# Blocked-cache attention on one core: K in loads of eight units, one more unit of lead for the scores, and a new order of copies and loads

## The chip, the core and the metric

The kernel runs on one core of one Trainium2 chip. The core has five engines with a queue of their own each: TensorE (PE; the profile shows its weight loads apart, as PEld), VectorE (DVE), ScalarE (ACT), GpSimd (POOL) and SyncE (SP), and 16 DMA engines beside them. In this kernel SP issues every transfer. TensorE works through its queue in order: an instruction that waits holds back all that stand behind it. The metric is the time of one launch in microseconds (us) on the device. Of each kernel there are several timed runs, whose median counts, and one execution that was profiled.

## What is computed

Two attention problems, A and B, of the same sizes, whose outputs are joined along the last axis:

```python
# B, Sq, D = 16, 144, 448;  H, Sk, Dh = 16, 512, 256;  bfloat16
q = (x @ wq).reshape(B, Sq, H, Dh).transpose(0, 2, 1, 3)
scores = einsum("bhqd,bhkd->bhqk", q, k_cache) * Dh ** -0.5
p = softmax(scores, axis=-1)
o = einsum("bhqk,bhkd->bhqd", p, v_cache)
out_A = o.transpose(0, 2, 1, 3).reshape(B, Sq, H * Dh) @ wo
```

Each of the 2 x 16 x 16 = 512 pairs of batch and head is called a unit here, numbered U = 0 to 511.

## The kernel before

A Python loop over a step number i writes out the program of every engine by hand. A small class, `_Sched`, keeps for each tile who wrote and read it last and puts in the waits. One step holds the stages of several units, each ahead of the last stage by a fixed lead: at step i the loop emits Q of unit i + LQ, the scores of unit i + LS, the transposes of unit i + LT, and PV of unit i. LQ is 22, LS is 13, LT is 2. The stages of a unit are:

- `t_q` (L333): eight TensorE matmuls make q, transposed, in the PSUM tile qp_ps; DVE or ACT scales it into qt_sb (L345, L349).
- 144 query rows do not fit 128 partitions. Rows 0 to 111 (QA) of each unit are its main part; the last 32 rows of four units together are one "remainder" block of 128 rows. `t_sb` (L359) makes the remainder's scores of eight units at once, in the two tiles sb_ps, at every eighth step (phase 0, where (i + 14) % 8 is 0).
- `t_sa` (L435): two matmuls of 512 columns make the main part's scores of one unit in sa_ps. There are two such tiles, each one PSUM bank.
- Softmax of the main part: DVE takes the negated maximum from sa_ps (`t_max`, L446); ACT takes the exponential from sa_ps with the row sum (`t_exp`, L457, an ACTIVATE and an ACTIVATION_READ_ACCUMULATOR); one step later DVE takes the reciprocal (L467) and POOL normalises P (`t_norm`, L475).
- `t_ta` (L488): four PE transposes turn P of one unit around. They write to the same two PSUM tiles as the scores, under the name pta_ps, bitcast to bfloat16; DVE copies them to pt_sb (`t_evac_pta`, L498).
- The remainder's P is normalised on POOL (L400), transposed by a DMA from pb_sb to pbt_sb (`t_ptb_dma`, L410, called pb below), and copied by POOL into pt_sb (`t_copy_ptb`, L421), four units at a time.
- `t_pv` (L521): eight matmuls with V; ACT copies the result into a ring of output columns (L536, L538).
- `t_op_piece` (L559): the output projection, in chunks of 128 rows, two matmuls a piece, is queued behind PV as a chunk becomes complete and spread over the steps by a credit counter; it starts at step OP_FROM of each problem.

Which of the two score tiles a stage uses is said by the unit's number alone, and the main loop of a step emits them in this order:

```python
bank = U % 2        # in t_sa, t_max, t_exp, and also in t_ta and t_evac_pta
...
u = i + LS          # then t_sa(u), t_max(u), t_exp(u)
u = i + LS - 1      # then t_recip(u), t_norm(u)
u = i + LT          # then t_ta(u), t_evac_pta(u)
```

On TensorE a step is so: Q, (every eighth step the remainder's scores), SA, TA, PV, OP.

Transfers are planned in a list, `dma_plan`, of (step, function); they are emitted on SP's one queue when the loop gets to that step, and wait there in order. K comes by transposing DMAs of four units (1 MB) into one of four slots (`t_load_k`, L309); V by loads of four units into one of five slots (L318); x for two batches (L289, L290; the first batch alone ahead, L299, L300); Wq in four parts (L267, L269) and Wo in eight (L277) for each problem. A K slot is free when the scores of its last unit are done.

Of the kernel before, what the change touches and what calls it, by code (L numbers as in the profile page):

```python
# [5 lines left out]
BF16 = mybir.dt.bfloat16  # L6
# [6 lines left out]
PE, ACT, DVE, POOL, SP = "pe", "act", "dve", "pool", "sp"  # L13
# [109 lines left out]
def bass_concat_heads__mha_block_cached__gqa_block_cached__near_ridge_kernel(  # L123
# [13 lines left out]
    xs = (A_x, B_x)  # L137
    ks = (A_k_cache, B_k_cache)
# [4 lines left out]
    Bn, SQ, D = A_x.shape  # L143
    H, SK, DH = A_k_cache.shape[1], A_k_cache.shape[2], A_k_cache.shape[3]
# [3 lines left out]
    NU = Bn * H  # L148
    NT = NP * NU
# [8 lines left out]
    NWG = NWO // WOG  # L158
    NPC = NWO // OPP

    LQ, LS, LT = 22, 13, 2
    LSB = 14
    NKH, NV, NXG = 4, 5, 2
    WO_AT = ((10, 21), (21, 25))
    OP_FROM = (22, 26)
    XB = 2
    assert Bn % XB == 0
    NQT, NPA, NPB, NPT, NST, NSTB, NOST = 12, 13, 2, 8, 4, 2, 3
    NPBT = 1
    RS = 4  # L170
    RC = RS * 128
# [7 lines left out]
    with contextlib.ExitStack() as es:  # L179
        def sb(name, shape, dt):  # L180
            return es.enter_context(nc.sbuf_tensor(name, shape, dt))
# [4 lines left out]
        wq_sb = sb("wq_sb", [128, 4, H * DH], BF16)  # L186
        wo_sb = sb("wo_sb", [128, NWO, D], BF16)
        ring = sb("ring", [128, NWO, RC], BF16)
        kt_sb = sb("kt_sb", [128, NKH, 2, 4 * SK], BF16)
        v_sb = sb("v_sb", [128, NV, 4, 4 * DH], BF16)  # L190
        xt_sb = sb("xt_sb", [128, NXG, 4, XB * SQ], BF16)
        qt_sb = sb("qt_sb", [128, NQT, 2, SQ], BF16)
# [13 lines left out]

        S = _Sched()
        sem_names = list(COMPUTE)
        for i in range(NKH):
# [5 lines left out]
        sem_names.append("xf")  # L215
        for i in range(HG):
            sem_names.append("wq%d" % i)
        for i in range(NWG):
# [63 lines left out]
        def t_load_x(XG):  # L282
            pr, j = divmod(XG, Bn // XB)
            sl = XG % NXG
            x = xs[pr][j * XB:(j + 1) * XB].rearrange("b q d -> (b q) d")
            o = SQ if XG == 0 else 0

            def e(q):
                q.dma_start_transpose(xt_sb[:, sl, 0:3, o:XB * SQ], x[o:XB * SQ, 0:384]).then_inc(sems["xt%d" % sl], 16)  # L289
                return q.dma_start_transpose(xt_sb[:, sl, 3, o:XB * SQ], x[o:XB * SQ, 320:448]).then_inc(  # L290
                    sems["xt%d" % sl], 16)
            S.add(SP, e, writes=[(("xt", sl, f), XG) for f in range(2) if XG > 0 or f > 0], dma_sem="xt%d" % sl,
                  n_dma=2, name="x%d" % XG)

        def t_load_x_first():
            x = xs[0][0]

            def e(q):
                q.dma_start_transpose(xt_sb[:, 0, 0:3, 0:SQ], x[:, 0:384]).then_inc(sems["xf"], 16)  # L299
                return q.dma_start_transpose(xt_sb[:, 0, 3, 0:SQ], x[:, 320:448]).then_inc(sems["xf"], 16)  # L300
            S.add(SP, e, writes=[(("xt", 0, 0), 0)], dma_sem="xf", n_dma=2, name="xf")

        def t_load_k(KH):
            pr, r0 = divmod(4 * KH, NU)
            sl = KH % NKH
            src = ks[pr].rearrange("b h k d -> (b h k) d")[r0 * SK:(r0 + 4) * SK, :]

            def e(q):
                return q.dma_start_transpose(kt_sb[:, sl, :, :], src).then_inc(sems["kt%d" % sl], 16)  # L309
            S.add(SP, e, writes=[(("kt", sl), KH)], dma_sem="kt%d" % sl, name="k%d" % KH)  # L310

        def t_load_v(G):
            pr, b, h0 = unit(4 * G)
# [7 lines left out]
        def t_q(U):  # L321
            pr, b, h = unit(U)
            XG = (pr * Bn + b) // XB
            xsl = XG % NXG
            xo = (b % XB) * SQ
            hg = h // 4

            def e(t):
                ins = None
                for kc in range(4):  # L330
                    for dc in range(2):
                        c0 = h * DH + dc * 128
                        ins = t.matmul(qp_ps[:, dc * SQ:(dc + 1) * SQ], lhsT=wq_sb[:, kc, c0:c0 + 128],  # L333
                                       rhs=xt_sb[:, xsl, kc, xo:xo + SQ], start=(kc == 0 and dc == 0),
                                       stop=(kc == 3), skip_group_check=True)
                return ins
            S.add(PE, e, reads=[(("wq", hg), pr), ("wqz", 0), (("xt", xsl, min(b % XB, 1)), XG)], writes=[("qp", ("q", U))],
                  banks=["qp"], name="Q%d" % U)

        def t_evac_q(U):  # L340
# [11 lines left out]
        def t_sb(SG):  # L352
            def e(t):
                ins = None
                for dc in range(2):
                    for jj in range(8):
                        U = 8 * SG + jj
                        j = jj % 4
                        ins = t.matmul(sb_ps[jj // 4][32 * j:32 * j + 32, :], lhsT=qt_sb[:, U % NQT, dc, QA:SQ],  # L359
                                       rhs=kt_sb[:, (U // 4) % NKH, dc, j * SK:(j + 1) * SK], start=(dc == 0),  # L360
                                       stop=(dc == 1), tile_position=(0, 32 * j))
                return ins
            S.add(PE, e, reads=[(("qt", (8 * SG + jj) % NQT), 8 * SG + jj) for jj in range(8)] +
                  [(("kt", KH % NKH), KH) for KH in (2 * SG, 2 * SG + 1)],
                  writes=[(("sbb", 0), ("s", 2 * SG)), (("sbb", 1), ("s", 2 * SG + 1))], banks=["sb0", "sb1"],
                  name="SB%d" % SG)

# [56 lines left out]
                  name="cptb%d" % G)  # L424

        def t_sa(U):
            KH = U // 4
            ksl = KH % NKH
            bank = U % 2
            ko = (U % 4) * SK  # L430

            def e(t):
                ins = None
                for dc in range(2):
                    ins = t.matmul(sa_ps[bank][0:QA, :], lhsT=qt_sb[:, U % NQT, dc, 0:QA],  # L435
                                   rhs=kt_sb[:, ksl, dc, ko:ko + SK], start=(dc == 0), stop=(dc == 1))
                return ins
            S.add(PE, e, reads=[(("qt", U % NQT), U), (("kt", ksl), KH)], writes=[(("sap", bank), ("s", U))],
                  banks=["sa%d" % bank], name="SA%d" % U)

        def t_max(U):
# [161 lines left out]
        def plan_k(at, KH):  # L603
            plan(at, 4 * (KH - NKH) + 3 - LS + 1 if KH >= NKH else s_min, 8 * (KH // 2) - LSB, t_load_k, KH)

        def plan_v(at, G):
            plan(at, 4 * (G - NV) + 3 + 1 if G >= NV else s_min, 4 * G, t_load_v, G)

        def plan_pb(at, SG):
            plan(at, 8 * SG - LSB + 5, 8 * SG - 1, t_ptb_dma, SG)  # L610

        plan(s_min, s_min, -LQ, t_load_x_first)
        for hg in range(HG):
            plan(s_min + (1 if hg < 2 else 3), s_min, 4 * hg - LQ, t_load_wq, 0, hg)
        for KH in range(2):
            plan_k(s_min + 2, KH)
        plan(s_min + 4, s_min, H - LQ, t_load_x, 0)
        for KH in range(2, 4):
            plan_k(s_min + 5, KH)
        plan_v(s_min + 6, 0)  # L620
        plan_v(s_min + 6, 1)
        plan_v(-5, 2)
        for pr in range(NP):
            for wg in range(NWG):
                plan(pr * NU + WO_AT[pr][wg // 4], s_min, pr * NU + OP_FROM[pr] + wg, t_load_wo, pr, wg)
        for n in range(0, NSG, 2):
            t = 8 * n
            XG = (t + 32) // (XB * H)
            if (t + 32) % (XB * H) == 0 and XG < NXGT:
                plan(t - 4, (XG - 1) * XB * H - LQ, XG * XB * H - LQ, t_load_x, XG)  # L630
            plan_pb(t - 4, n)
            if n + 2 < NSG:
                plan_k(t - 3, 2 * n + 4)
                plan_k(t - 3, 2 * n + 5)
                plan_k(t + 2, 2 * n + 6)
            plan_pb(t + 2, n + 1)
            if n + 2 < NSG:
                plan_k(t + 4, 2 * n + 7)
            for j, at in enumerate((5, 5, 5, 8)):
                if 2 * n + 3 + j < NG:  # L640
                    plan_v(t + at, 2 * n + 3 + j)
        for hg in range(HG):
            dl = NU + 4 * hg - LQ
            lo = NU - H + 4 * hg + 3 - LQ + 1
            plan((8, 9, 10, 12)[hg] + NU - 32, lo, dl, t_load_wq, 1, hg)
        dma_plan.sort(key=lambda t: t[:2])

        u_tail0 = NT - H
# [32 lines left out]
        while True:  # L681
# [28 lines left out]
            if 0 <= u < NT:  # L710
                t_sa(u)
                t_max(u)
                t_exp(u)
            u = i + LS - 1
            if 0 <= u < NT:
                t_recip(u)
# [6 lines left out]
                t_max_b(ga)  # L723
            if ok and ph == 2:
                t_max_b(gb)
            if i % 8 == 7 and 0 <= i + 1 < NT:
                t_copy_ptb((i + 1) // 4)
            if i % 8 == 1 and 0 <= i < NT:
                t_copy_ptb((i + 3) // 4)
            u = i  # L730
            if 0 <= u < NT:
                t_pv(u)
# [91 lines left out]
```

## Time and profile before

| What | Value |
|---|---|
| Median of 3 runs | 1253.64 us (1253.57 to 1255.31) |
| The profiled execution's own time | 1255.94 us |
| Its span in the trace | 1254.2 us, mean granted TensorE clock 0.985 |
| PE busy | 1175.2 us, 94% of the span |
| DVE, ACT, POOL busy | 732.0, 750.4, 727.9 us (58 to 60%) |
| Matmuls | 13440, the same number of weight loads |
| DMA | 310.89 MB, mean 248 GB/s, q1 at 105.1% of 16 engines' span |

The span is what the trace covers from the first to the last instruction; the time of the run is 1.7 us longer. Busy times are sums of the records of one engine; matmuls are pipelined and their ends are modelled, so a record's length is not the time until the next matmul may start. Starts are measured, so the prediction works with distances between starts. A row of the timeline gives start, length, engine, line, operation, output<-input and, in brackets, idle time ahead of it with what ended it.

### The profile page before, as it was taken

How to read it: one execution, taken by the hardware profiler on the slowest of the kernel's cores; microseconds unless marked ns; L12 is line 12 of the kernel's file. 1: busy time of each engine (PE TensorE's matmuls, PEld its weight loads, DVE VectorE, ACT ScalarE, POOL GpSimd, SP SyncE). 2: the span in 40 equal slices, each digit the busy share in tenths (PEclk: the TensorE clock that was granted, in tenths of full speed). 3: DMA queues.
4: the chain of work that ended last, by engine and by line, in shares of the span. 5: the costliest groups of instructions: out<-in, count | busy, mean ns of one | idle time of the engine just before them, and what ended most of it. 6: DMA issues, size and time to landing. Idle time of an engine off the chain costs nothing.

```text
span 1254.2 us, 32874 instructions
## 1 busy us (share of the span) xinstructions
PE 1175.2 (94%) x13440; PEld 881.6 (70%) x13440; DVE 732.0 (58%) x2051; ACT 750.4 (60%) x2213; POOL 727.9 (58%) x774
## 2 busy tenths in 40 slices
PE   5698999999999999999799989999999999999989
PEld 3466777777777777777577757777777777777766
DVE  2464566665666666566465546656665665666662
ACT  2464566666666566566466646656666666666662
POOL 0564656666666566566465636656666665666661
PEclk9898999999999999999899989999999999999999
DMA  9999999999999999999999999999999999999961
GB/s 212 249 282 289 242 242 266 264 267 260 263 238 224 258 271 236 266 262 245 272 259 267 260 261 270 241 259 254 241 236 266 262 252 262 262 222 243 254 185 54
DMA packets 700695, 310.89 MB, mean 248 GB/s; under 512 B 618624, under 2 KB 631424, under 8 KB 700544
## 3 DMA queue, kind: packets, MB, share of 16 engines
q1 hardware_dynamic: 700544, 308.78, 105.1%
q8 instruction: 106, 1.74, 0.6%
q14 instruction: 45, 0.37, 0.1%
HBM read 148.90 MB, written 4.13 MB: 122 GB/s over the span
## 4 chain that ended last, share of the span: by engine, by line
PE 73%; POOL 7%; DVE 7%; issue 5%; DMA 4%; SPq 3%; ACT 1%; DVEq 0%
PE ot_ps L521 17%; PE op_ps L559 16%; PE qp_ps L333 15%; PE sa_ps L435 14%; PE sa_ps L488 5%; PE sb_ps L359 5%; POOL pa_sb L475 5%; POOL pt_sb L421 3%; DMA kt_sb<-in_A_k_cache_dram 2%; DVE qt_sb L345 2%; SPq L309 2%; DVE stat L446 2%; DMA pbt_sb<-pb_sb 2%; DVE stat L467 1%; DVE pt_sb L498 1%
## 5 line engine op out<-in xcount | busy, mean ns | idle before, releaser
L475 POOL TENSOR_TENSOR pa_sb<-pa_sb,stat 112x512 bf16<-112x512 bf16 x512 | 532.1, 1039 | 469.5 <-DVE stat L467 467.9
L457 ACT ACTIVATE pa_sb<-sa_ps,stat 112x512 bf16<-112x512 f32 x512 | 351.8, 687 | 425.8 <-DVE stat L446 424.0
L446 DVE TENSOR_REDUCE stat<-sa_ps 112x1 f32<-112x512 f32 x512 | 354.0, 691 | 386.8 <-PE sa_ps L435 381.4
L333 PE MATMUL qp_ps<-xt_sb,wq_sb 128*128 128x144 bf16 x4096 | 347.8, 229 | 26.2 <-DMA wq_sb<-in_A_wq_dram 9.4
L521 PE MATMUL ot_ps<-pt_sb,v_sb 128*128 128x144 bf16 x4096 | 344.5, 227 | 29.1 <-POOL pt_sb L421 29.1
L333 PEld LDWEIGHTS qp_ps<-xt_sb,wq_sb 128*128 128x128 bf16 x4096 | 291.3, 99 | 104.8 <-issue 18.7
L435 PE MATMUL sa_ps<-kt_sb,qt_sb 128*112 128x512 bf16 x1024 | 315.0, 390 | 4.5 <-DVE pt_sb L498 3.1
L521 PEld LDWEIGHTS ot_ps<-pt_sb,v_sb 128*128 128x128 bf16 x4096 | 268.9, 98 | 37.7 <-POOL pt_sb L421 37.1
L559 PE MATMUL op_ps<-wo_sb,ring 128*128 128x448 bf16 x1120 | 275.5, 354 | 0.0
L488 PEld LDWEIGHTS sa_ps<-ident,pa_sb 112*128 112x128 bf16 x2048 | 161.0, 114 | 107.4 <-ACT pa_sb L457 28.2
L536 ACT ACTIVATE ring<-ot_ps 128x288 bf16<-128x288 f32 (+8 forms) x512 | 190.1, 371 | 21.0 <-PE ot_ps L521 21.0
L498 DVE COPY pt_sb<-sa_ps 128x448 bf16<-128x448 bf16 x512 | 190.9, 373 | 14.0 <-PE sa_ps L488 14.0
L488 PE MATMUL sa_ps<-ident,pa_sb 112*128 112x112 bf16 x2048 | 187.6, 214 | 0.4 <-ACT pa_sb L457 0.4
L345 DVE TENSOR_SCALAR qt_sb<-qp_ps 128x288 bf16<-128x288 f32 x256 | 117.0, 457 | 109.6 <-PE qp_ps L333 109.4
L400 POOL TENSOR_TENSOR pb_sb<-pb_sb,stat 128x512 bf16<-128x512 bf16 x128 | 133.0, 1039 | 27.7 <-DVE stat L392 27.7
L349 ACT ACTIVATE qt_sb<-qp_ps 128x288 bf16<-128x288 f32 x256 | 105.7, 413 | 52.7 <-PE qp_ps L333 51.0
L435 PEld LDWEIGHTS sa_ps<-kt_sb,qt_sb 128*112 128x112 bf16 x1024 | 97.3, 131 | 44.6 <-issue 28.4
L559 PEld LDWEIGHTS op_ps<-wo_sb,ring 128*128 128x128 bf16 x1120 | 96.5, 98 | 32.9 <-issue 0.4
L457 ACT ACTIVATION_READ_ACCUMULATOR pa_sb<-sa_ps,stat 112x1 f32 x512 | 98.8, 193 | 0.0
L372 DVE TENSOR_REDUCE stat<-sb_ps 128x1 f32<-128x512 f32 x128 | 87.2, 681 | 3.6 <-PE sb_ps L359 3.6
L382 ACT ACTIVATE pb_sb<-sb_ps,stat 128x512 bf16<-128x512 f32 x128 | 88.3, 690 | 0.0
L359 PE MATMUL sb_ps<-kt_sb,qt_sb 128*32 128x512 bf16 x1024 | 70.8, 399 | 15.9 <-DMA kt_sb<-in_A_k_cache_dram 12.0
(20 smaller groups left out, 297.0 us busy)
## 6 DMA issues: line engine op xcount, KB each, us to landing
v_sb<-in_A_v_cache_dram SPq DMA_DIRECT2D x64, 1024.0 KB, 8.8
v_sb<-in_B_v_cache_dram SPq DMA_DIRECT2D x64, 1024.0 KB, 8.4
out_dram<-ost_sb SPq DMA_DIRECT2D x36, 112.0 KB, 8.4
wo_sb<-in_A_wo_dram SPq DMA_DIRECT2D x8, 448.0 KB, 7.3
wo_sb<-in_B_wo_dram SPq DMA_DIRECT2D x8, 448.0 KB, 7.5
wq_sb<-in_A_wq_dram SPq DMA_DIRECT2D x4, 768.0 KB, 6.4
wq_sb<-in_B_wq_dram SPq DMA_DIRECT2D x4, 768.0 KB, 10.3
kt_sb<-in_A_k_cache_dram SPq DMA_TRANSPOSE x64, 7.8
```

The source lines that it names most:

```text
L333: ins = t.matmul(qp_ps[:, dc * SQ:(dc + 1) * SQ], lhsT=wq_sb[:, kc, c0:c0 + 128], rhs=xt_sb[:, xsl, kc, xo:xo + SQ], start=(kc == 0 and dc ...
L345: return v.tensor_scalar(qt_sb[:, sl, :, :], src, 1.0 / 16.0, None, op0=ALU.mult)
L359: ins = t.matmul(sb_ps[jj // 4][32 * j:32 * j + 32, :], lhsT=qt_sb[:, U % NQT, dc, QA:SQ], rhs=kt_sb[:, (U // 4) % NKH, dc, j * SK:(j + 1) ...
L435: ins = t.matmul(sa_ps[bank][0:QA, :], lhsT=qt_sb[:, U % NQT, dc, 0:QA], rhs=kt_sb[:, ksl, dc, ko:ko + SK], start=(dc == 0), stop=(dc == 1))
L446: return v.tensor_reduce(stat[0:QA, NEG + sl:NEG + sl + 1], sa_ps[bank][0:QA, :], axis=AX.X, op=ALU.max, negate=True)
L457: return a.activation(pa_sb[0:QA, psl, :], sa_ps[bank][0:QA, :], AF.Exp, bias=stat[0:QA, NEG + sl:NEG + sl + 1], scale=1.0, accum_out=stat ...
L475: return g.tensor_tensor(pa_sb[0:QA, psl, :], pa_sb[0:QA, psl, :], stat[0:QA, RINV + sl:RINV + sl + 1].to_broadcast([QA, SK]), op=ALU.mult)
L488: ins = t.transpose(pta_ps[bank][:, c * 128:c * 128 + QA], src[:, c, :], ident[0:QA, 0:QA])
L498: return v.tensor_copy(pt_sb[:, sl, :, 0:QA], pta_ps[bank][:, 0:512].rearrange("p (c q) -> p c q", c=4)[:, :, 0:QA])
L521: ins = t.matmul(ot_ps[ob][:, dc * SQ:(dc + 1) * SQ], lhsT=v_sb[:, vsl, j, c * DH + dc * 128:c * DH + (dc + 1) * 128], rhs=pt_sb[:, sl, c, ...
L536: ins = a.activation(ring[:, 2 * h:2 * h + 2, c0:c0 + n1], src[:, :, 0:n1], AF.Copy)
L559: ins = t.matmul(acc[0:m, 0:D], lhsT=ring[:, c, col0:col0 + m], rhs=wo_sb[:, c, :], start=(c == first), stop=(c == last))
```

## The change

- The lead of the main part's scores goes from 13 to 14 steps (LS), and the buffers of P from 13 to 14 (NPA).
- K comes in loads of eight units (2 MB) into two slots, in place of four units into four slots.
- Within a step, POOL's copy of the remainder's P (`t_copy_ptb`) is emitted ahead of the reciprocal and the normalisation.
- At the start, x of the first two batches comes in one load; K is issued as one load each at two places; the first three V loads stand behind the first remainder's P transposing DMA (pb), which is issued earlier.
- Wo comes at steps 21 and 37 of each problem (before: 10 and 21, 21 and 25), and the output projection starts at step 34 (before: 22 and 26).
- Wq of problem B is planned at 5, 5, 8 and 11 steps of the group before it is used (before: 8, 9, 10, 12), so that two of its parts stand ahead of a V load.

The core of the diff:

```diff
-    LQ, LS, LT = 22, 13, 2
+    LQ, LS, LT = 22, 14, 2
     LSB = 14
-    NKH, NV, NXG = 4, 5, 2
-    WO_AT = ((10, 21), (21, 25))
-    OP_FROM = (22, 26)
+    NK, NV, NXG = 2, 5, 2
+    WO_AT = ((21, 37), (21, 37))
+    OP_FROM = (34, 34)
...
-        kt_sb = sb("kt_sb", [128, NKH, 2, 4 * SK], BF16)
+        kt_sb = sb("kt_sb", [128, 2, NK * 8 * SK], BF16)
...
+        def t_load_k(SG):
+            pr, r0 = divmod(8 * SG, NU)
+            sl = SG % NK
+            src = ks[pr].rearrange("b h k d -> (b h k) d")[r0 * SK:(r0 + 8) * SK, :]
+
+            def e(q):
+                return q.dma_start_transpose(kt_sb[:, :, sl * 8 * SK:(sl + 1) * 8 * SK], src).then_inc(
+                    sems["kt%d" % sl], 16)
+            S.add(SP, e, writes=[(("kt", sl), SG)], dma_sem="kt%d" % sl, name="k%d" % SG)
...
-        plan(s_min, s_min, -LQ, t_load_x_first)
+        plan(s_min, s_min, -LQ, t_load_x, 0)
...
-        for KH in range(2):
-            plan_k(s_min + 2, KH)
-        plan(s_min + 4, s_min, H - LQ, t_load_x, 0)
-        for KH in range(2, 4):
-            plan_k(s_min + 5, KH)
-        plan_v(s_min + 6, 0)
-        plan_v(s_min + 6, 1)
-        plan_v(-5, 2)
+        plan_k(s_min + 2, 0)
+        plan_k(s_min + 4, 1)
+        for G in range(3):
+            plan_v(-7, G)
...
-            plan_pb(t - 4, n)
+            plan_pb(t - 4 if n else -8, n)
             if n + 2 < NSG:
-                plan_k(t - 3, 2 * n + 4)
-                plan_k(t - 3, 2 * n + 5)
-                plan_k(t + 2, 2 * n + 6)
+                plan_k(t - 3, n + 2)
             plan_pb(t + 2, n + 1)
             if n + 2 < NSG:
-                plan_k(t + 4, 2 * n + 7)
+                plan_k(t + 2, n + 3)
...
-            plan((8, 9, 10, 12)[hg] + NU - 32, lo, dl, t_load_wq, 1, hg)
+            plan((5, 5, 8, 11)[hg] + NU - 32, lo, dl, t_load_wq, 1, hg)
...
                 t_exp(u)
+            if i % 8 == 7 and 0 <= i + 1 < NT:
+                t_copy_ptb((i + 1) // 4)
+            if i % 8 == 1 and 0 <= i < NT:
+                t_copy_ptb((i + 3) // 4)
             u = i + LS - 1
             if 0 <= u < NT:
                 t_recip(u)
...
-            if i % 8 == 7 and 0 <= i + 1 < NT:
-                t_copy_ptb((i + 1) // 4)
-            if i % 8 == 1 and 0 <= i < NT:
-                t_copy_ptb((i + 3) // 4)
```

More of the change, by code (lines that the diff above doesn't have):

```diff
@@ L159, in bass_concat_heads__mha_block_cached__gqa_block_cached__near_ridge_kernel @@
     NPC = NWO // OPP
-    LQ, LS, LT = 22, 13, 2
+    LQ, LS, LT = 22, 14, 2
     LSB = 14
-    NKH, NV, NXG = 4, 5, 2
-    WO_AT = ((10, 21), (21, 25))
-    OP_FROM = (22, 26)
+    NK, NV, NXG = 2, 5, 2
+    WO_AT = ((21, 37), (21, 37))
+    OP_FROM = (34, 34)
     XB = 2
     assert Bn % XB == 0
-    NQT, NPA, NPB, NPT, NST, NSTB, NOST = 12, 13, 2, 8, 4, 2, 3
+    NQT, NPA, NPB, NPT, NST, NSTB, NOST = 12, 14, 2, 8, 4, 2, 3
     NPBT = 1
@@ L208, in bass_concat_heads__mha_block_cached__gqa_block_cached__near_ridge_kernel @@
         sem_names = list(COMPUTE)
-        for i in range(NKH):
+        for i in range(NK):
             sem_names.append("kt%d" % i)
@@ L214, in bass_concat_heads__mha_block_cached__gqa_block_cached__near_ridge_kernel @@
             sem_names.append("xt%d" % i)
-        sem_names.append("xf")
         for i in range(HG):
@@ L285, in t_load_x @@
             x = xs[pr][j * XB:(j + 1) * XB].rearrange("b q d -> (b q) d")
-            o = SQ if XG == 0 else 0
             def e(q):
[L289 to L296, printed above, removed]
-            def e(q):
[L299 to L310, printed above, removed]
+                q.dma_start_transpose(xt_sb[:, sl, 0:3, :], x[:, 0:384]).then_inc(sems["xt%d" % sl], 16)
+                return q.dma_start_transpose(xt_sb[:, sl, 3, :], x[:, 320:448]).then_inc(sems["xt%d" % sl], 16)
+            S.add(SP, e, writes=[(("xt", sl), XG)], dma_sem="xt%d" % sl, n_dma=2, name="x%d" % XG)
+        def t_load_k(SG):
+            pr, r0 = divmod(8 * SG, NU)
+            sl = SG % NK
+            src = ks[pr].rearrange("b h k d -> (b h k) d")[r0 * SK:(r0 + 8) * SK, :]
+            def e(q):
+                return q.dma_start_transpose(kt_sb[:, :, sl * 8 * SK:(sl + 1) * 8 * SK], src).then_inc(
+                    sems["kt%d" % sl], 16)
+            S.add(SP, e, writes=[(("kt", sl), SG)], dma_sem="kt%d" % sl, name="k%d" % SG)
         def t_load_v(G):
@@ L336, in e @@
                 return ins
-            S.add(PE, e, reads=[(("wq", hg), pr), ("wqz", 0), (("xt", xsl, min(b % XB, 1)), XG)], writes=[("qp", ("q", U))],
+            S.add(PE, e, reads=[(("wq", hg), pr), ("wqz", 0), (("xt", xsl), XG)], writes=[("qp", ("q", U))],
                   banks=["qp"], name="Q%d" % U)
@@ L359, in e @@
                         ins = t.matmul(sb_ps[jj // 4][32 * j:32 * j + 32, :], lhsT=qt_sb[:, U % NQT, dc, QA:SQ],
-                                       rhs=kt_sb[:, (U // 4) % NKH, dc, j * SK:(j + 1) * SK], start=(dc == 0),
+                                       rhs=kt_sb[:, dc, (U % (8 * NK)) * SK:(U % (8 * NK) + 1) * SK], start=(dc == 0),
                                        stop=(dc == 1), tile_position=(0, 32 * j))
@@ L363, in t_sb @@
             S.add(PE, e, reads=[(("qt", (8 * SG + jj) % NQT), 8 * SG + jj) for jj in range(8)] +
-                  [(("kt", KH % NKH), KH) for KH in (2 * SG, 2 * SG + 1)],
+                  [(("kt", SG % NK), SG)],
                   writes=[(("sbb", 0), ("s", 2 * SG)), (("sbb", 1), ("s", 2 * SG + 1))], banks=["sb0", "sb1"],
@@ L426, in t_sa @@
         def t_sa(U):
-            KH = U // 4
-            ksl = KH % NKH
+            SG = U // 8
+            ksl = SG % NK
             bank = U % 2
-            ko = (U % 4) * SK
+            ko = (U % (8 * NK)) * SK
             def e(t):
@@ L435, in e @@
                     ins = t.matmul(sa_ps[bank][0:QA, :], lhsT=qt_sb[:, U % NQT, dc, 0:QA],
-                                   rhs=kt_sb[:, ksl, dc, ko:ko + SK], start=(dc == 0), stop=(dc == 1))
+                                   rhs=kt_sb[:, dc, ko:ko + SK], start=(dc == 0), stop=(dc == 1))
                 return ins
-            S.add(PE, e, reads=[(("qt", U % NQT), U), (("kt", ksl), KH)], writes=[(("sap", bank), ("s", U))],
+            S.add(PE, e, reads=[(("qt", U % NQT), U), (("kt", ksl), SG)], writes=[(("sap", bank), ("s", U))],
                   banks=["sa%d" % bank], name="SA%d" % U)
@@ L601, in plan, with plan_k @@
             dma_plan.append((at, len(dma_plan), fn, args))
-        def plan_k(at, KH):
-            plan(at, 4 * (KH - NKH) + 3 - LS + 1 if KH >= NKH else s_min, 8 * (KH // 2) - LSB, t_load_k, KH)
+        def plan_k(at, SG):
+            plan(at, 8 * (SG - NK) + 7 - LS + 1 if SG >= NK else s_min, 8 * SG - LSB, t_load_k, SG)
         def plan_v(at, G):
```

## The prediction

> **What bounds the kernel now.** I read the page first, then the waits, the timeline of one steady stretch, and windows around TensorE's pauses.
>
> ```profile
> PE 1175.2 (94%) x13440; PEld 881.6 (70%) x13440; DVE 732.0 (58%) x2051; ACT 750.4 (60%) x2213; POOL 727.9 (58%) x774
> ```
>
> TensorE is the bound and the others have over 40% to spare. So a change pays by what it takes off TensorE's in-order queue, and costs by what it makes that queue wait for. The waits view names what TensorE lost:
>
> ```profile
> PEld ot_ps L521 <- POOL pt_sb L421: 37.1, 57, 3.2
> PE ot_ps L521 <- POOL pt_sb L421: 29.1, 57, 3.1
> PEld sa_ps L488 <- ACT pa_sb L457: 28.2, 101, 0.8
> PE sb_ps L359 <- DMA kt_sb<-in_A_k_cache_dram: 12.0, 4, 5.1
> PEld sa_ps L435 <- DVE pt_sb L498: 9.3, 26, 0.6
> PE qp_ps L333 <- issue: 8.5, 1, 8.5
> PE sb_ps L359 <- DMA kt_sb<-in_B_k_cache_dram: 3.4, 1, 3.4
> ```
>
> The copy of the remainder's P is worth 29.1 us, late K 15.4, late Wq 8.5: these are what the new order of loads and copies can win. The third row matters most: transposes (TA, L488) wait for the exponential of ACT (L457) because both use the two score banks. In the timeline, first a step where TA need not wait, then one where it does:
>
> ```profile
> 844.61 0.59 PE L435 MATMUL sa_ps<-kt_sb,qt_sb 128*112 128x512 bf16 x2
> 845.05 0.36 PE L488 MATMUL sa_ps<-ident,pa_sb 112*128 112x112 bf16 x4
> 845.25 0.69 DVE L446 TENSOR_REDUCE stat<-sa_ps 112x1 f32<-112x512 f32 x1
> ...
> 850.96 0.69 DVE L446 TENSOR_REDUCE stat<-sa_ps 112x1 f32<-112x512 f32 x1 [0.66 <-PE sa_ps L435]
> 851.68 0.69 ACT L457 ACTIVATE pa_sb<-sa_ps,stat 112x512 bf16<-112x512 f32 x1 [0.40 <-DVE stat L446]
> 852.27 0.19 ACT L457 ACTIVATION_READ_ACCUMULATOR pa_sb<-sa_ps,stat 112x1 f32 x1
> 852.51 0.25 PEld L488 LDWEIGHTS sa_ps<-ident,pa_sb 112*128 112x128 bf16 x4 [0.27 <-ACT pa_sb L457]
> 852.54 0.37 PE L488 MATMUL sa_ps<-ident,pa_sb 112*128 112x112 bf16 x4
> 852.74 0.67 PE L521 MATMUL ot_ps<-pt_sb,v_sb 128*128 128x144 bf16 x8
> ```
>
> From SA's start TA follows in 0.44 us (844.61 to 845.05). The chain behind one SA is: 0.64 to its maximum (844.61 to 845.25), 0.72 to the exponential (850.96 to 851.68), 0.83 to the weights of the TA that waits for it (851.68 to 852.51), 0.03 to its matmul: 2.22 us. Today that chain spans two steps, so only its last 0.27 us shows.
>
> **The lead of 14.** This number decides. At step i TensorE does SA of unit i+LS, then TA of unit i+2, in bank U % 2. With LS 13 the two units differ in parity: TA goes into the bank whose scores were made a step ago. With 14 they have the same parity: TA(i+2) must go into the bank that SA(i+14) has just filled, and cannot until DVE and ACT have read those scores. TensorE is in order, so PV, the projection, the next Q and SA all stand behind it. The 2.22 us now lie within one step, in place of 0.43 (0.44 and 0.43 in the neighbouring steps): +1.79 per step. It holds for steps -2 to 497, 500 of them (the last scores are at 497): 500 x 1.79 = **+895 us**. Bounds: rows of one kind differ by up to 0.05 (SA's own 0.59 or 0.64, say), at two links of the chain 0.1 a step (-50 us); if ACT or DVE is still at another row when its turn comes, as much the other way (+50). I take 2.22, as in the chain above: DVE's Q scaling (0.46) and the remainder's exponential (0.69 and 0.20) end before the scores do.
>
> **What the stall swallows.** A step that takes nearly 4 us hides what was late before. POOL's copy: -29.1. The copy moves ahead of the normalisation, but LS moves the normalisation by one unit too, so on POOL the copy for units 0 to 3 still stands between the normalisations of units 11 and 12; what it gains is a step of TensorE's time, over 2 us against waits of mostly 0.5. The old waits of TA (-28.2) and of SA for the DVE copy (-9.3) vanish, since the other bank has long been free. They are PEld rows whose cost in starts I take whole; at the least nothing of them (+37).
>
> **K in eights.** No bytes change. SP is busy 13.49 us for three 4-unit loads (4.5 each), and they land 7.8 us after issue (median, DMA issues): 3.3 behind the 4.5. Eight units: 9.0 + 3.3 = 12.3 us. A slot is free at step 8n-7 and needed at 8n+2: nine steps, 35 us at the new pace (20 at the old 2.27). Behind a K load on SP stand the next pb and V; pb needs to land only by step 8n+7. So K waits fall by 15.4 less the first (1.38 at 39 us): -14.0; at the worst every one of the 62 later loads waits as long as the longest of before, 62 x 5.1 = +316, which needs a landing three times slower. I take -14.
>
> **The start.** x as one load holds Wq back by at most one transpose's row (1.3 us); SP is freed of two later ones (2.6), so the second K comes about that much earlier, while TensorE paces itself on Q until 38 us anyway. pb no longer stands behind V and x (issued at 46.1 though its data were ready at 34); V behind it has until step 0. Between -3 and +2, taken as 0.
>
> **Wo and Wq.** Wo's loads (8.4 us of SP for four) move, and the projection starts at step 34: its 1152 matmuls remain and the credit counter catches up before the end: 0. Steps 22 to 33 only lose cover for TensorE's clock. Wq of B is issued five steps, 20 us, ahead against a landing of 10.3: -8.5, or 0 if it is late as before.
>
> **The clock.** PEclk is 0.50 in the profile's windows after pauses. Eleven windows at that clock hold 28.2 us of PE busy time; with no pause left, half of it goes: -14.1. But the new stall is a pause in each step. Do 1.6 us of idleness (2.22 less SA's own 0.6) every 3.9 us let the clock drop? Windows on the grid at which the clock changes; PE busy comes first, PEclk follows the POOL column:
>
> ```profile
> 48.79:52.20 3.41, 1.51 (x18) 0.90 (x15) 2.46 (x7) 1.56 (x4) 1.80 (x2) 1.00 1.41 160
> 52.20:55.62 3.42, 1.82 (x16) 1.82 (x17) 0.00 (x0) 0.41 (x1) 1.61 (x2) 0.50 1.29 254
> 137.54:140.95 3.41, 1.70 (x24) 1.32 (x21) 1.05 (x3) 2.33 (x7) 1.89 (x3) 1.00 1.19 268
> 140.95:144.36 3.41, 2.43 (x32) 1.56 (x33) 0.78 (x3) 0.05 (x1) 0.00 (x0) 1.00 1.18 246
> 734.87:738.28 3.41, 1.17 (x15) 0.99 (x16) 0.54 (x3) 1.19 (x3) 1.61 (x2) 1.00 1.07 205
> 738.28:741.70 3.42, 3.42 (x24) 2.50 (x22) 1.05 (x3) 1.49 (x4) 1.06 (x2) 0.50 1.13 213
> ```
>
> A window busy for 1.51 (44%) or 1.17 (34%) was followed by half the clock; one busy for 1.70 (50%) was not. The shortest new step, without projection, is 2.22 + 0.20 + 0.50 + 0.50 = 3.42, so a window of 3.41 holds one pause at most: 3.41 - 1.62 = 1.79 busy, 52%. The clock should stay, by a thin margin.
>
> The Trainium skill speaks against this pattern: "TensorE: Matmul & The Clock Gate", section "A second HAM failure mode: psum-queue depth-cycling", tells of a kernel that cycles PSUM banks, whose short idle spells between groups of matmuls make the clock swing. By that rule the time would lie with the second rival below. The same page (Part 1) wants an idle window of some 3.4 us before the clock halves; by that the full clock would hold; but here it halved after a pause of 2.6 us (734.5 to 737.1), so the measured shares decide.
>
> **The sum.** Span 1254.2 + 895 - 29.1 - 28.2 - 9.3 - 14.0 - 8.5 - 14.1 = 2046. Second way, from starts: a step is 2.22 + 0.20 (TA to PV) + 0.50 (PV on) + 0.50 (Q to SA) + 2.13 projection matmuls x 0.19 + 0.98/8 for the remainder's scores = 3.94; 500 x 3.94 = 1970, plus 45.8 before step -2 and 27.2 from the last SA on, as before: 2043. I take a span of 2045. The run's time is 1.7 over its span and the median 2.3 under that run, so the median should be about 2045 too.
>
> **Rivals.**
> - *Half clock, some or all of the time* (0.15). For: 52% is near the 44% that failed. Against: the 50% that held. In cold rows a step is 2.67 (1.09 to the maximum) + 0.37 + 0.96 + 0.96 + 2.13 x 0.37 + 0.23 = 5.98: fully cold 45.8 + 2990 + 27.2 = 3063; half the time 2550; a tenth 2147.
> - *K late* (0.02): the waits of +316 above, about 2360, if a load of eight takes more than the nine steps.
> - *Not slower: TA does not meet the fresh scores* (0.03). If the order on TensorE let the exponential end before TA comes up, as now, only the gains would stand: 1254 - 29 - 14 - 8.5 - 14 = 1188. It decides where TA's wait is on the exponential of the unit before, not of the unit just scored; `bank = U % 2` with leads 14 and 2 says otherwise. A stall of 0.13 us a step would just eat the 66 us of gains; above that the kernel is slower.
> - The forecast, full clock: 0.80, with own bounds of about 1990 to 2140 (the sums of the bounds above).
>
> **Range and chances.** 1990 to 2300 takes in the forecast's bounds and the clock lost for up to a quarter of the time. About 0.2%, 2.5 us, is what a measurement here can tell from no change. Faster 0.02, same 0.01, slower 0.97.
>
> **What would show it.** After the change, PE's wait for ACT L457 at L488 should be the longest of TensorE, some 500 times at 1.6 us, about 800 us; start of SA to start of TA 2.2 us in every step; PE about 55 to 60% busy; waits for POOL L421 and K near zero; PEclk 1.00 but at the start. If TA waits less than 1 us a step, the parity argument is wrong; if PEclk shows 0.5 in many slices, the clock argument is.

## The result, and the profile after

The changed kernel takes 2059.38 us (median of 4 runs, 2058.26 to 2060.94). The kernel before, run beside it, took 1253.61 us (median of 4, 1252.59 to 1255.31). The ratio is 1.643, with a 95% interval of 1.640 to 1.646. So 806 us were added; the prediction said 2045, in a range of 1990 to 2300.

In the changed kernel the line numbers are smaller by about eleven: the scores (SA) are L424, their maximum L435, the exponential L446, the transposes (TA) L477, PV L510, POOL's copy L410, K's load L297. First the page: busy shares, the granted clock in 40 slices, and the shares of the chain that ended last.

```profile
PE 1237.3 (60%) x13440; PEld 842.1 (41%) x13440; DVE 788.1 (38%) x2051; ACT 839.7 (41%) x2213; POOL 736.6 (36%) x774
PEclk9999999999999999999999999999999999999998
PE 54%; DVE 24%; ACT 19%; issue 2%; DMA 0%; SPq 0%; POOL 0%; DVEq 0%
```

TensorE has the same 13440 matmuls, but fills 60% of the span in place of 94%. Its clock is at full speed in nearly every slice. The chain of waits now runs through DVE (24%) and ACT (19%), which held 7% and 1% of it before; POOL and DMA, at 7% and 4% before, have gone from it. The waits view says where TensorE stands:

```profile
PE sa_ps L477 <- ACT pa_sb L446: 799.4, 500, 1.6
PE qp_ps L322 <- DMA wq_sb<-in_A_wq_dram: 9.3, 1, 9.3
PE qp_ps L322 <- ACT qt_sb L338: 4.1, 7, 0.7
```

One wait, 500 times, 1.6 us each, 799.4 us together. No row of this view names POOL's copy, a load of K, or Wq of problem B any more; the second row is the start of the kernel, as before (9.4). One step in the timeline shows what the wait consists of (rows of the chain only):

```profile
1002.33 0.59 PE L424 MATMUL sa_ps<-kt_sb,qt_sb 128*112 128x512 bf16 x2
1002.96 0.69 DVE L435 TENSOR_REDUCE stat<-sa_ps 112x1 f32<-112x512 f32 x1 [1.04 <-PE sa_ps L424]
1003.69 0.69 ACT L446 ACTIVATE pa_sb<-sa_ps,stat 112x512 bf16<-112x512 f32 x1 [0.75 <-DVE stat L435]
1004.28 0.19 ACT L446 ACTIVATION_READ_ACCUMULATOR pa_sb<-sa_ps,stat 112x1 f32 x1
1004.52 0.39 PE L477 MATMUL sa_ps<-ident,pa_sb 112*128 112x112 bf16 x4 [1.60 <-ACT pa_sb L446]
```

Scores at 1002.33, maximum at 1002.96, exponential at 1003.69, transposes at 1004.52: 2.19 us from SA's start to TA's. Over the whole trace the mean of the 500 distances is 2.20. TensorE idles 1.60 of it, between two stages that do not even belong to the same unit.

The clock is shown by stretches laid on the grid at which it changes (PE busy first, PEclk behind the POOL column). First a window of the steady part, then the first one that cost the clock:

```profile
72.02:75.43 3.41, 1.81 (x25) 1.35 (x23) 1.96 (x6) 1.96 (x6) 1.17 (x2) 1.00 1.06 395
48.13:51.54 3.41, 1.34 (x15) 0.86 (x14) 2.07 (x6) 0.78 (x2) 1.38 (x2) 1.00 1.04 173
51.54:54.95 3.41, 2.28 (x21) 2.29 (x22) 0.72 (x3) 1.19 (x3) 1.59 (x2) 0.50 1.29 233
```

The steady window is busy for 1.81 of 3.41 us, 53%. There are some 310 windows of 52 to 53% in the trace and after none of them did the clock drop. It dropped twice: at 51.54, after a window of 39%, and at 2010.80, again after 39%.

### The profile page after: what moved, and what is told of

It reads as the page before. It is cut to its first block, busy times and chain, and to the rows that moved or that the text cites. A ratio compares the mean times of both kernels' runs of the same rounds, so it can differ in the third digit from the quotient of the medians.

```text
span 2057.1 us, 32478 instructions
## 1 busy us (share of the span) xinstructions
PE 1237.3 (60%) x13440; PEld 842.1 (41%) x13440; DVE 788.1 (38%) x2051; ACT 839.7 (41%) x2213; POOL 736.6 (36%) x774
## 4 chain that ended last, share of the span: by engine, by line
PE 54%; DVE 24%; ACT 19%; issue 2%; DMA 0%; SPq 0%; POOL 0%; DVEq 0%
ACT pa_sb L446 19%; DVE stat L435 17%; PE qp_ps L322 12%; PE ot_ps L510 12%; PE op_ps L548 10%; PE sa_ps L477 10%; PE sa_ps L424 6%; DVE qt_sb L334 6%; PE sb_ps L348 3%; DVE stat L361 1%; DVE pt_sb L487 1%; PE qp_ps L548 0%; DMA wq_sb<-in_A_wq_dram 0%; ACT qt_sb L338 0%; ACT pb_sb L371 0%
## 5 line engine op out<-in xcount | busy, mean ns | idle before, releaser
L477 PE MATMUL sa_ps<-ident,pa_sb 112*128 112x112 bf16 x2048 | 199.3, 220 | 799.4 <-ACT pa_sb L446 799.4
L446 ACT ACTIVATE pa_sb<-sa_ps,stat 112x512 bf16<-112x512 f32 x512 | 352.6, 689 | 560.3 <-DVE stat L435 559.8
L477 PEld LDWEIGHTS sa_ps<-ident,pa_sb 112*128 112x128 bf16 x2048 | 127.1, 118 | 1032.4 <-ACT pa_sb L446 1030.4
L435 DVE TENSOR_REDUCE stat<-sa_ps 112x1 f32<-112x512 f32 x512 | 354.2, 692 | 429.9 <-PE sa_ps L424 429.9
L487 DVE COPY pt_sb<-sa_ps 128x448 bf16<-128x448 bf16 x512 | 200.6, 392 | 634.1 <-PE sa_ps L477 634.1
L525 ACT ACTIVATE ring<-ot_ps 128x288 bf16<-128x288 f32 (+8 forms) x512 | 195.6, 382 | 513.6 <-PE ot_ps L510 513.6
L510 PE MATMUL ot_ps<-pt_sb,v_sb 128*128 128x144 bf16 x4096 | 343.7, 227 | 0.0
L424 PE MATMUL sa_ps<-kt_sb,qt_sb 128*112 128x512 bf16 x1024 | 309.9, 384 | 0.0
L510 PEld LDWEIGHTS ot_ps<-pt_sb,v_sb 128*128 128x128 bf16 x4096 | 271.0, 98 | 0.4
L424 PEld LDWEIGHTS sa_ps<-kt_sb,qt_sb 128*112 128x112 bf16 x1024 | 98.4, 131 | 27.2 <-issue 27.2
L446 ACT ACTIVATION_READ_ACCUMULATOR pa_sb<-sa_ps,stat 112x1 f32 x512 | 99.0, 193 | 0.0
L410 POOL COPY pt_sb<-pbt_sb 128x512 bf16<-128x512 bf16 x128 | 78.0, 609 | 13.8 <-PE ot_ps L510 13.8
```

The source lines that it names most:

```text
L435: return v.tensor_reduce(stat[0:QA, NEG + sl:NEG + sl + 1], sa_ps[bank][0:QA, :], axis=AX.X, op=ALU.max, negate=True)
L446: return a.activation(pa_sb[0:QA, psl, :], sa_ps[bank][0:QA, :], AF.Exp, bias=stat[0:QA, NEG + sl:NEG + sl + 1], scale=1.0, accum_out=stat ...
L477: ins = t.transpose(pta_ps[bank][:, c * 128:c * 128 + QA], src[:, c, :], ident[0:QA, 0:QA])
L487: return v.tensor_copy(pt_sb[:, sl, :, 0:QA], pta_ps[bank][:, 0:512].rearrange("p (c q) -> p c q", c=4)[:, :, 0:QA])
L510: ins = t.matmul(ot_ps[ob][:, dc * SQ:(dc + 1) * SQ], lhsT=v_sb[:, vsl, j, c * DH + dc * 128:c * DH + (dc + 1) * 128], rhs=pt_sb[:, sl, c, ...
L525: ins = a.activation(ring[:, 2 * h:2 * h + 2, c0:c0 + n1], src[:, :, 0:n1], AF.Copy)
```

## The experiments

Ratios are to the kernel before, run on the same chip in turn. Each diff is against the kernel that its first line names.

### Which part costs the time

**The lead alone.** Is the whole loss in the one number?

```diff
(kernel before)
-    LQ, LS, LT = 22, 13, 2
+    LQ, LS, LT = 22, 14, 2
...
-    NQT, NPA, NPB, NPT, NST, NSTB, NOST = 12, 13, 2, 8, 4, 2, 3
+    NQT, NPA, NPB, NPT, NST, NSTB, NOST = 12, 14, 2, 8, 4, 2, 3
```

> The kernel before with one number changed: the lead of the scores goes from 13 to 14 (and the buffers of P from 13 to 14, which the lead needs). K stays in fours, and no load and no copy moves. Parity theory: 500 steps stall as in the changed kernel, SA to TA 2.2 us, TensorE waits for ACT at the transposes some 500 times for 800 us in all; about 2060 us, within 30 of the changed kernel's 2059. Rival, the loads of eight units or the order on SP cost the time: about 1254, as before.

Measured: 2066.69 us (2061.07 to 2068.91), ratio 1.645 (1.640 to 1.651). TensorE waits for the exponential at TA 500 times, 798.5 us together, as in the full change. Loads, copies and Wq of the change are not in this kernel, so the lead makes the whole loss. The wait for POOL's copy is gone here too, although the copy was not moved: at this pace it is the stall that hides it. The worth of the other edits at this pace (2067 against 2059) lies within the overlap of the two intervals.

**The changed kernel with the other bank for TA.** The lead of 14 stays; only the tile that TA writes and DVE copies from is swapped.

```diff
(kernel after; the same line in t_ta and in t_evac_pta)
-            bank = U % 2
+            bank = (U + 1) % 2
```

> The changed kernel with the transposes (and DVE's copy out of them) in the other of the two score banks: bank = (U + 1) % 2 in these two functions, all else as changed, the lead of 14 and K in eights included. Parity theory: the stall of 1.6 us in each step goes, what the other edits win stays: 1188 by the prediction's sum, 1180 to 1230. TensorE's waits for POOL's copy and for K are near zero, its clock is full but for the start and the end. Rival, a lead of 14 or loads of eight are themselves late: above 1254, with TensorE waiting for K or for Q.

Measured: 1230.33 us (1227.68 to 1232.52), ratio 0.980 (0.977 to 0.983). One line in two places takes 829 us away, and the time lies at the upper edge of what was expected. In the timeline TA now follows SA by 0.43 us, while the scores just made still wait for DVE (other rows left out):

```profile
845.54 0.59 PE L424 MATMUL sa_ps<-kt_sb,qt_sb 128*112 128x512 bf16 x2
845.97 0.36 PE L477 MATMUL sa_ps<-ident,pa_sb 112*128 112x112 bf16 x4
846.17 0.69 DVE L435 TENSOR_REDUCE stat<-sa_ps 112x1 f32<-112x512 f32 x1 [0.89 <-PE sa_ps L424]
```

So the bank is the cause, not the lead as a distance. But the time is 42 us above the 1188 that the prediction gave for "only the gains would stand". The waits view names where they are:

```profile
PE sb_ps L348 <- DMA kt_sb<-in_B_k_cache_dram: 11.3, 5, 5.3
PE sb_ps L348 <- DMA kt_sb<-in_A_k_cache_dram: 11.0, 7, 5.4
...
PE ot_ps L510 <- POOL pt_sb L410: 7.1, 2, 5.5
PE qp_ps L322 <- issue: 5.2, 1, 5.2
```

K's waits are 22.3 us, more than the 15.4 of before, not gone. POOL's copy still costs 7.1, Wq of B 5.2. In the terms of the prediction's sum: copy -22.0 (29.1 to 7.1), K +6.9, Wq -3.3, and PE busy 9.1 lower (1175.2 to 1166.1). That is -27.5, against a span that fell by 25.3. The clock is little of it: 25.2 us of PE's busy time lie at half clock here, 28.2 in the kernel before, so the clock gives 1.5 us where the sum had 14.1. The 9.1 lies in PV: its share of PE's busy time, each moment counted once, falls from 270.1 to 259.4 us, and to 258.9 in the kernel below where the copy alone is moved, so it belongs to the copy more than to the clock.

**The lead of 14 with the other bank, alone.**

```diff
(kernel before, with LS and NPA of 14 as above; in t_ta and t_evac_pta)
-            bank = U % 2
+            bank = (U + 1) % 2
```

> The kernel before with the lead of 14 and the transposes in the other bank; loads and copy as before. Parity theory: neither stall nor gain, since the copy still stands behind a normalisation that is one unit later: 1245 to 1258. Rival, the longer lead itself pays (or costs) by giving softmax one more step: more than 10 us away from 1254.

Measured: 1258.01 us (10 runs, 1255.07 to 1262.29), ratio 1.002 (1.000 to 1.004). One more unit of lead, taken without the bank clash, gains nothing and costs 0.4% at most. POOL's copy costs 30.3 us in 57 waits, as before: it is not the lead that helps the copy.

**The other parity by the other lead.** TA one step earlier makes the leads differ by 11 rather than 12, with the banks untouched.

```diff
(kernel after)
-    LQ, LS, LT = 22, 14, 2
+    LQ, LS, LT = 22, 14, 3
```

> The changed kernel with the transposes three steps ahead of PV in place of two: the leads 14 and 3 differ by an odd number, so the banks differ again, with no change to the bank's formula. Parity theory: as with the other bank, 1180 to 1230. Rival, what counts is the distance in steps between scores and transposes (now 11, before 11, changed 12): also near 1190, but then the kernel with 12 steps and the other bank must be slow, so the two are told apart together.

Measured: 1228.94 us (1226.87 to 1231.14), ratio 0.979 (0.975 to 0.983), the same as with the swapped bank. Both leads may move; what must stay odd is their difference.

### What the rest of the change is worth at the old pace

**The early copy alone.**

```diff
(kernel before)
                 t_exp(u)
+            if i % 8 == 7 and 0 <= i + 1 < NT:
+                t_copy_ptb((i + 1) // 4)
+            if i % 8 == 1 and 0 <= i < NT:
+                t_copy_ptb((i + 3) // 4)
             u = i + LS - 1
...
-            if i % 8 == 7 and 0 <= i + 1 < NT:
-                t_copy_ptb((i + 1) // 4)
-            if i % 8 == 1 and 0 <= i < NT:
-                t_copy_ptb((i + 3) // 4)
             u = i
```

> The kernel before with one edit: POOL's copy of the remainder's P is emitted ahead of the reciprocal and the normalisation of its step; lead 13, loads as before. On POOL the copy for units 0 to 3 now stands ahead of the normalisation of unit 11 in place of behind it. Forecast: most of the 29.1 us that TensorE waited for the copy goes, less the three long waits at 54, 93 and 737 us, which are for the DMA ahead of the copy (7 us): 1228 to 1240. Rival, the copy waits for the DMA anyway: 1250 to 1256.

Measured: 1229.89 us (1227.31 to 1229.92), ratio 0.980 (0.978 to 0.982). TensorE's wait for the copy falls from 57 times and 29.1 us to this:

```profile
PE ot_ps L521 <- POOL pt_sb L421: 6.5, 3, 2.4
```

The wait is 22.6 us shorter, nearly all of the 24.7 gained, and the time is within what was expected. This one edit gains as much as the whole change does with its bank clash taken out (ratio 0.980 both).

**The changed kernel with the other bank, and the copy put back.** What is left is the lead (worth nothing by itself), the loads of eight, and the new places of V, Wo and Wq.

```diff
(kernel after, with the swapped bank as above)
-            if i % 8 == 7 and 0 <= i + 1 < NT:
-                t_copy_ptb((i + 1) // 4)
-            if i % 8 == 1 and 0 <= i < NT:
-                t_copy_ptb((i + 3) // 4)
             u = i + LS - 1
...
+            if i % 8 == 7 and 0 <= i + 1 < NT:
+                t_copy_ptb((i + 1) // 4)
+            if i % 8 == 1 and 0 <= i < NT:
+                t_copy_ptb((i + 3) // 4)
             u = i
```

> The changed kernel with the transposes in the other bank and the copy put back behind the normalisation: what is left of the change are the loads and the lead. Forecast: TensorE's waits of mostly 0.5 us for the copy return, 55 to 60 of them, so 20 to 30 us above the kernel with the other bank alone; K, Wq and Wo waits stay away, so 20 to 45 us below 1254. Rival, the early copy brings nothing once pb is early: as the kernel with the other bank.

Measured: 1263.58 us (1259.73 to 1267.48), ratio 1.007 (1.005 to 1.010). The expectation missed, on the other side of no change: without the early copy the new loads cost 9 us. Its waits for the copy are back, and K waits longer than before:

```profile
PE ot_ps L510 <- POOL pt_sb L410: 26.6, 45, 4.5
PE sb_ps L348 <- DMA kt_sb<-in_A_k_cache_dram: 16.9, 8, 5.2
PE sb_ps L348 <- DMA kt_sb<-in_B_k_cache_dram: 8.8, 6, 2.6
```

The waits for K are 25.7 us against 15.4; these 10.3 us are about the loss. The traces show that K has less to spare here. From the moment when a K slot is free (its last scores are done) to the remainder's scores that need the new load there are 20.6 us here and 26.1 in the kernel before (medians), because a slot of eight units is free only when all eight are done. A load of eight lands 11.6 us after issue, one of four 7.8. With the time that a load waits for its turn on SP, K lands 3.5 us ahead of its use here and 8.2 before (medians). The 13 loads that TensorE waited for by more than 0.3 us were issued 7 to 17 us after their slot was free, against a median of 3.8 for all. No kernel changed the loads of K alone, so how much the size costs by itself stays open.

**The early copy and the early Wq**, without the loads of eight.

```diff
(kernel before, with the early copy as above)
-            plan((8, 9, 10, 12)[hg] + NU - 32, lo, dl, t_load_wq, 1, hg)
+            plan((5, 5, 8, 11)[hg] + NU - 32, lo, dl, t_load_wq, 1, hg)
```

> The kernel before with the early copy (as in the run with the copy alone, 1230) and Wq of problem B planned at 5, 5, 8 and 11 as in the changed kernel; lead 13, K in fours, Wo as before. By the prediction's step: TensorE's 8.2 us wait for Wq near 598 us and the half clock behind it (about 2 us) go: 1218 to 1224. Rival, Wq is late for lack of transfer time and not for its place on SP (with the other bank it still waited 5.2 us): 1225 to 1232.

Measured: 1223.76 us (1223.37 to 1228.63) against 1251.6 for the kernel before on this chip; ratio 0.978 (0.976 to 0.980). By the ratio it is the fastest kernel of this study, faster than both kernels compared here, but its interval overlaps that of the early copy alone. TensorE's wait at Wq of B is 5.0 in place of 8.2, and the wait for K 20.7 in place of 18.6: what Wq may have won is about what K lost. The time lies in the expected 1218 to 1224, but this chip also runs the kernel before some 3 us faster than those of the earlier runs; the ratio would give 1227 there, which is the rival's range, and Wq was still waited for.

**Wo later as well.**

```diff
(the kernel just above)
-    WO_AT = ((10, 21), (21, 25))
-    OP_FROM = (22, 26)
+    WO_AT = ((21, 37), (21, 37))
+    OP_FROM = (34, 34)
```

> As the one above, with Wo at steps 21 and 37 and the projection from step 34 as well: all edits of the change but the lead, K in eights and the first loads. Forecast: Wo no longer stands ahead of the K loads that were waited for at 99, 142 and 733 us (5.4, 5.2, 3.0 us, and the half clock behind them): 6 to 15 us below the one above. Rival, the transfers are only moved against other loads, K waits as long elsewhere: within 4 us of it.

Measured: 1225.01 us (1223.33 to 1231.01), ratio 0.980 (0.977 to 0.982). The waits for K are 19.0 (20.7 without this edit), those for the copy 7.1 (4.4). They only change places; no gain can be told from none, as the rival had it.

### How near the clock was to halving

Both kernels add an instruction to the chain that TA waits for: a second maximum by DVE on the same scores, into spare columns of stat, whose result nothing uses. It lengthens the pause and takes no work from TensorE.

**A full second maximum** (512 columns).

```diff
(kernel after, in t_max, ahead of the maximum; stat has NST columns more)
+            def e0(v):
+                return v.tensor_reduce(stat[0:QA, XTR + sl:XTR + sl + 1], sa_ps[bank][0:QA, :], axis=AX.X,
+                                       op=ALU.max)
+            S.add(DVE, e0, reads=[(("sap", bank), ("s", U))], writes=[(("xtr", sl), U)], banks=["sa%d" % bank],
+                  name="xtr%d" % U)
```

> The changed kernel with one more maximum over the same scores on DVE (0.69 us, into a column that nobody reads) ahead of the one that the exponential needs: the chain from SA to TA grows from 2.2 to 2.9 us and the pause from 1.6 to 2.3. Chain theory, clock full: 500 x 0.69 = 345 us more, about 2400. Clock theory: a window of 3.41 us can then hold a whole pause and be busy for only 1.1 us (33%), below the 44% that cost the clock; at half clock a step is 6.65 us, and by the shares of windows that would lose and regain it some 60% of the time would be cold: about 2900, 2700 to 3100, with PEclk near 0.7 over the whole page. If DVE's time were not on the path: about 2060.

Measured: 2945.44 us (2941.69 and 2949.19), ratio 2.35 (2.34 to 2.36). The page's clock row and the wait:

```profile
PEclk8778676677667676676676777686777677777677
PE sa_ps L484 <- ACT pa_sb L453: 1096.7, 500, 2.2
```

The 500 waits grew by 297 us (to 2.19 each), the time by 886. The other 589 us are TensorE's own work at half clock, which holds in 57% of the time: PE is busy for 1818.3 us, 581 more than in the changed kernel. So the expected 2700 to 3100 was met. Four windows on the grid:

```profile
210.24:213.65 3.41, 1.22 (x21) 1.18 (x21) 1.75 (x4) 1.08 (x4) 1.82 (x3) 1.00 0.01 2
213.65:217.07 3.42, 1.23 (x8) 0.39 (x6) 1.81 (x4) 0.94 (x3) 0.85 (x1) 0.51 0.00 0
...
220.48:223.89 3.41, 1.43 (x21) 1.36 (x22) 1.57 (x4) 1.19 (x4) 1.59 (x2) 0.99 0.00 0
223.89:227.31 3.42, 1.23 (x16) 0.84 (x15) 1.75 (x4) 1.19 (x3) 1.04 (x1) 1.00 0.73 120
```

With 1.22 us busy (36%) the next window is at half clock; with 1.43 us (42%) it is not. In the whole trace the clock dropped 234 times, always behind a window of at most 43%, and it stayed full behind some two dozen windows of 42 to 47%. So the rival "half clock" was a real one: 0.59 us more in each pause brings it about.

**A short second maximum** (128 columns).

```diff
(the kernel just above)
-                return v.tensor_reduce(stat[0:QA, XTR + sl:XTR + sl + 1], sa_ps[bank][0:QA, :], axis=AX.X,
+                return v.tensor_reduce(stat[0:QA, XTR + sl:XTR + sl + 1], sa_ps[bank][0:QA, 0:128], axis=AX.X,
```

> The changed kernel with a short extra maximum on DVE (128 of the 512 columns, into a column that nobody reads) ahead of the one that the exponential needs. The whole extra maximum added 0.59 us to the pause; by columns this one adds about 0.19, so the pause is 1.79 us and a window of 3.41 us that holds one is busy for 1.62, 47.5%: between the 39 to 44% that lost the clock and the 50 to 52% that kept it. If the bound lies below 47%: 500 x 0.19 = 95 more, about 2155, with PEclk 0.99. If it lies above: half clock for much of the time, as with the longer chain, 2450 to 2800.

Measured: 2180.77 and 2214.69 us in two runs, with a mean granted clock of 0.980 and 0.958. The 500 waits come to 897.4 us (1.79 each, +0.19), which accounts for 98 us. The trace is of the longer run. The rest of its excess (156 us over the changed kernel's own profiled run) goes with the clock: at half in 8.5% of the span, more than half of that in two stretches near the start. The shorter run lost clock too, by its mean of 0.980 (0.993 in the changed kernel). Neither forecast fits: the time is above 2155 and far below 2450. Windows with one pause are busy for 47%. Of some 240 such windows at full clock 15 were followed by half the clock, such as the second one shown here, at 170.17:

```profile
132.62:136.03 3.41, 1.61 (x23) 1.26 (x22) 1.75 (x5) 1.11 (x3) 1.59 (x2) 1.00 0.00 0
136.03:139.45 3.42, 1.62 (x23) 1.17 (x21) 1.35 (x4) 1.40 (x5) 1.04 (x1) 1.00 0.68 121
...
170.17:173.58 3.41, 1.61 (x22) 0.70 (x15) 0.96 (x3) 0.88 (x3) 1.04 (x1) 1.00 1.28 289
173.58:176.99 3.41, 2.49 (x18) 1.65 (x15) 2.33 (x6) 1.09 (x3) 0.00 (x0) 0.52 1.28 290
```

The same 1.61 us were enough at 132.62 and too little at 170.17. And 42% was enough at 220.48 in the kernel with the full second maximum. So no single share of modelled busy time separates windows that lose the clock from those that keep it: from 42 to 47% both happen. Why is not shown.

## Why the prediction was right

**The lead.** The step that decided holds to within 1%: 500 waits of 1.6 us were forecast as "about 800 us" and measure 799.4. From SA to TA it said 2.22 us and the mean is 2.20; a step without projection was to take 3.42, and in the stretch from 67.50 to 77.76 us three steps take 3.42 each. The lead alone gives 2067, the other bank 1230, the other lead 1229: the parity of the two leads makes the loss.

**What the stall swallows.** At the new pace the waits for POOL's copy, for K and for Wq of B are gone from the view, as the sum had it, and so are those of SA for DVE. With the lead alone, where the copy was not moved, its wait is gone as well: the longer step is enough for it, as the prediction said. The order of Wo and Wq and the start cost nothing that shows; step -2 begins at 44.12 us, 1.7 earlier than taken.

**The clock.** It kept full speed in the steady part, by the margin named: windows of 52 to 53% held. The two experiments with a longer chain put the margin's lower end between 42 and 47%, as far as modelled ends of matmuls can tell. But the term of -14.1 was mis-sized. The prediction let every pause vanish; in fact the clock still halves at both ends of the kernel (51.5 to 61.8 us, 2010.8 to 2027.9 us), behind windows whose steps lack PV or Q. Such a step is 2.92 us long, 0.50 shorter than the shortest that was counted with, so that a window of 3.41 us can hold more than one pause and be busy for 39% only. 18.7 us of PE's busy time lie at half clock there (28.2 before): the gain was 4.8 and not 14.1.

**What is left of the 12 us** between 2045 and the span of 2057.1. In the first way of adding, one more term was mis-sized: -28.2 for the old waits of TA. Those rows are of weight loads; TensorE's matmuls waited 0.4 us there. By starts, SA to TA took 0.452 us on average in the kernel before, against the 0.43 taken, so 11 us over 500 steps were there to win and not 28. The prediction allowed for that ("at the least nothing of them"). It is half made up by the chain (2.203 in place of 2.22, -8.5): SA to TA costs 875 us more in all, and the sum had 895 - 28.2 = 867. The clock adds its 9.3. In the second way, from starts, 44.1 us pass before step -2 (45.8 taken), 1977.1 from there to the last SA (1970), and 36.0 from the last SA on (27.2): 14 above 2043. In the steps TA to PV takes 0.225 us in place of 0.20, +12.5 over 500 steps. The end is longer than before because 18 more projection matmuls and one more unit's TA and PV come after the last SA, because the last SA is itself followed by a stall, and because the clock is at half for its first 6.7 us.

**The rivals.** "Half clock" fell, with the doubt in the right place. "K late" fell: K of eight units lands 11.1 to 11.5 us after issue (estimated 12.3), SP holds it for 8.3 (9.0), and no K is waited for. "Only gains" fell, and its price was wrong too: the kernel that removes the clash takes 1230, not 1188. The gain on POOL's copy is real and is nearly all there is. That on K is not one: at full pace K's waits grow from 15.4 to 22.3. The -14.0 for K was right only because the stall left 35 us for each load, and the -8.5 for Wq is 3.3 at full pace.

**The rule on the clock.** In the steady part a pause of 1.6 us in every step did not make the clock swing here, one of 1.8 did at times (half clock in 8.5% of the span), and one of 2.2 did so that it was at half in 57% of the time. The Trainium skill ("TensorE: Matmul & The Clock Gate", "A second HAM failure mode: psum-queue depth-cycling") tells of short idle spells between groups of matmuls that make the clock swing; these runs agree from the 1.8 us on. Its case is the prediction's rival "half clock", the first in the list, though the text there calls it the second. The same page's idle window of some 3.4 us (Part 1) is not what the clock asked for in these runs: windows 36% busy were enough to lose it.

## What to carry to other kernels

Where two stages take turns on the same two buffers, chosen by the unit's number, the difference of their leads decides whether a stage meets the buffer just filled or the one filled a step ago. Before a lead is changed by one, write out which buffer each stage uses in one step. A transfer's earlier place in the order was worth nothing here where the DMA was busy throughout; the wait moved to another transfer, while the one edit that paid removed a wait of TensorE on a compute engine. Before loads are made larger, count the time from a free slot to the use of the new data: a larger load gets its slot later and lands later.

## What the runs showed of the hardware

- The granted clock changes on a fixed grid of 3.41 us and mostly follows how busy TensorE was in the window just ended: 52 to 53% kept full clock in all of some 310 windows of the changed kernel; 47% kept it mostly (15 drops in some 240 windows, short second maximum); 42% kept it at 220.48 us in the kernel with the full second maximum, and there no window above 43% lost it; 39% and 36% lost it. The kernel before lost it once behind 44%. No gap as long as a window was needed.
- Full clock came back only after a window that was busy for most of its length. At half clock in the kernel with the full second maximum, a window of 94% (217.07 us) was followed by full clock, as were all from 80% on, and windows of up to 77% stayed at half. In the kernel with the short second maximum both happened at 82 to 83%. So a drop can last several windows: there one lasted from 173.6 to 221.4 us.
- A transposing load of 2 MB holds SP's queue for 8.3 us and lands 11.1 to 11.5 us after issue where the DMA has room (61% of the engines' time), 11.8 to 12.0 us at the old pace (median hold 9.3 us, with the other bank). A load of 1 MB held it for 4.6 us in the kernel before and landed 7.8 us after issue (medians).
